# Decode attention with the roles of the score matmul swapped: row-layout softmax in place of column-layout softmax, and one slot arena

## The chip, the cores and the metric

The kernel runs on one core of one Trainium2 chip. The metric is the device time of one execution in microseconds (us); lower is better. Every quoted time is the median of the executions of that kernel. A ratio is the mean time of one kernel's fast runs over that of the other's in the same rounds, so it is not quite the ratio of the medians quoted. The span of a trace is first to last instruction. Runs are "fast" if they lie within 1.5% of the fastest of the same kernel.

## The reference

```
x = A_x                                   # 4 batches, 1 token, D = 512
x = x + attention(layernorm(x))           # layer 0
x = x + glu(layernorm(x))                 # layer 1
x = x + attention(layernorm(x))           # layer 2, same K and V
x = x + glu(layernorm(x))                 # layer 3

attention: q = x @ wq                     # 32 query heads of 128, 8 KV heads
           k, v = the last 2048 positions of the caches, each KV head for 4 query heads
           p = softmax(q k^T / sqrt(128)); o = p v; return o @ wo
glu:       h = sigmoid(x @ w_gate) * (x @ w_up); return h @ w_down     # F = 1792
```

All tensors are bf16. One pair (batch, KV head) has a K block and a V block of 512 KB each, 32 of both. With four batches of one token, everything is matrix times a few columns, and 73.9 MB come from HBM (V twice, because the kernel keeps only K between the layers).

## The kernel before

The program lists logical operations with their reads and writes. A list scheduler with a cost model turns the list into one fixed order per engine, and semaphores are worked out from it. So the order on each engine is static: an engine that reaches an instruction whose input is missing waits, even if a later one could run.

K is loaded position-major and transposed on TensorE (PE) in layer 0. The transposed K stays in SBUF for layer 2. Buffers are: 32 places for transposed K, a place for the whole output projection, and an arena of 9 slots of 512 KB for everything else. In layer 2 a K place becomes a slot once its scores are done.

Scores in column layout: K^T is stationary, q moves (4 columns), so a block needs 16 weight loads and 16 tiny matmuls, and positions lie on partitions:

```
for j in range(NJ):                                   # 16 blocks of 128 positions
    c0 = b * NJ * REP + j * REP
    last = pe.matmul(ps[:, sbk, c0:c0 + REP],
                     kt[:, i * SLOT + j * 128: i * SLOT + (j + 1) * 128],       # stationary 128x128
                     qT[:, b * HQ + h * REP: b * HQ + (h + 1) * REP],           # 4 columns
                     start=True, stop=True)
# ... softmax across partitions, cut here: max over j (DVE), fp32 transpose (PE), max (DVE),
# broadcast (DVE), transpose back (PE), copy (ACT), subtract (DVE), exp (ACT) -> ebuf, sum (DVE),
# sum over partitions with a matrix of ones (PE), reciprocal (DVE)
for j in range(NJ):                                   # P times V
    last = pe.matmul(ps[:, OB, b * REP:(b + 1) * REP], src[:, j * 128:(j + 1) * 128],
                     ebuf[:, c0:c0 + REP], start=(j == 0), stop=(j == NJ - 1))
# ... scale by the reciprocal (DVE), output projection WO (16 matmuls), add to x (DVE)
```

Of the kernel before, what the change touches and what calls it, by code (L numbers as in the profile page):

```python
# [6 lines left out]
F32 = mybir.dt.float32  # L7
BF16 = mybir.dt.bfloat16
ACTF = mybir.ActivationFunctionType
ALU = mybir.AluOpType  # L10
# [234 lines left out]
class _SlotPool:  # L245

    def __init__(self, slots, est=None):
        self.free = [(s, ()) for s in slots]
        self.est = est

    def alloc(self):
        if not self.free:
            raise RuntimeError("slot pool exhausted (logical op order needs more slots)")
        if self.est is None:
            return self.free.pop(0)[0]
        best = 0
        best_t = None
        for k, (s, names) in enumerate(self.free):
            t = 0.0
            for n in names:  # L260
                v = self.est.get(n, 0.0)
                if v > t:
                    t = v
            if best_t is None or t < best_t - 1e-9:
                best, best_t = k, t
        return self.free.pop(best)[0]

    def release(self, s, names=()):
        self.free.append((s, tuple(names)))
# [3 lines left out]
    sem_lat=120.0, pick_tol=60.0,  # L273
    dma_issue=450.0, dma_lat0=900.0, dma_lat1=1100.0, dma_max_out=8,
    bw_4k=338.0, bw_1k=292.0, bw_8k=350.0,
    pe_pair=33.0, pe_tr=107.0, pe_small=230.0, pe_f32=590.0,
    dve_fix=70.0, dve_f32=1.04, dve_bf_psum=0.52,
    act_fix=70.0, act_el=0.833,
# [3 lines left out]
def build(nc, A_x, A_k, A_v, A_wq, A_wo, B_wg, B_wu, B_wd, out, cfg=None):  # L282
# [3 lines left out]
    NA = cfg.get("NA", 9)  # L286
    NE = cfg.get("NE", 4)
    ND = cfg.get("ND", 2)
# [11 lines left out]
    assert SQ == 1 and DH == 128 and D % 128 == 0 and W % 128 == 0 and F % 128 == 0  # L300
    assert HQ == HKV * REP and A_wq.shape[0] == D and A_wo.shape[0] == HQ * DH and A_wo.shape[1] == D
    SLOT = NJ * 128
    GC = NB * NJ * REP
    NR = NB * REP
    NX = NC * NB
    NBLK = NB * HKV
    TB = min(8, NJ)
    NHALF = NJ // TB
    assert NJ % TB == 0 and GC <= 512 and NR <= 128 and HQ * NB <= 512 and NFC * NB <= 512
    assert NB <= 32 and SLOT >= D  # L310
    SCALE = float(DH) ** -0.5
    EPS = 1e-5
    WOH = REP * D
    HQC = max(1, min(HQ, SLOT // 128))
    NQCH = (HQ + HQC - 1) // HQC
    GCW = max(128, min(F, (SLOT // 128) * 128))
    NGCH = (F + GCW - 1) // GCW
    FCC = max(1, SLOT // D)
    NDCH = (NFC + FCC - 1) // FCC

# [12 lines left out]
    with es:  # L333
        def sb(name, shape, dt):
            return es.enter_context(nc.sbuf_tensor(name, shape, dt))

        kt = sb("kt", [128, NBLK * SLOT], BF16)
        wo_sb = sb("wo_sb", [128, HKV * WOH], BF16)
        arena = sb("arena", [128, NA * SLOT], BF16)
        ident_b = sb("ident_b", [128, 128], BF16)  # L340
        ident_f = sb("ident_f", [128, 128], F32)
        ones_f = sb("ones_f", [128, 128], F32)
        x_nat = sb("x_nat", [NB, D], BF16)
        o_nat = x_nat
        xT = sb("xT", [128, NX], F32)
        xc = sb("xc", [128, NX], F32)
        sq = sb("sq", [128, NX], F32)
        xn = sb("xn", [128, NX], BF16)
        lnl = sb("lnl", [128, NB], F32)
        lr1 = sb("lr1", [128, NB], F32)  # L350
        lr2 = sb("lr2", [128, NB], F32)
        xb16 = sb("xb16", [128, NX], BF16)
        rstd = sb("rstd", [128, NB], F32)
        qT = sb("qT", [128, NB * HQ], BF16)
        m1 = sb("m1", [128, ND * NR], F32)
        gmv = sb("gmv", [NR, ND], F32)
        Gb = sb("Gb", [NR, ND * 128], F32)
        gbc = sb("gbc", [128, ND * NR], F32)
        dbuf = sb("dbuf", [128, ND * GC], F32)
        ebuf = sb("ebuf", [128, NE * GC], BF16)  # L360
        esum = sb("esum", [128, ND * NR], F32)
        rinv = sb("rinv", [128, NE * NR], F32)
        onb = sb("onb", [128, 2 * NR], BF16)
        eg = sb("eg", [128, NFC * NB], F32)
        sg = sb("sg", [128, NFC * NB], F32)
        hT = sb("hT", [128, NFC * NB], BF16)
        ps = es.enter_context(nc.psum_tensor("ps", [128, 8, 512], F32))
# [4 lines left out]
        slot_est = cfg.get("slot_est")  # L372
        for _pass in range(cfg.get("passes", 1)):
            P = _Plan()
            pool = _SlotPool(range(NA), slot_est)

            def slot_ap(s):
                if s < NA:
                    return arena[:, s * SLOT:(s + 1) * SLOT]
                i = s - NA  # L380
                return kt[:, i * SLOT:(i + 1) * SLOT]

            def slot_tok(s):
                if s < NA:
                    return (("slot", s),)
                i = s - NA
                return tuple(("kt", i, t) for t in range(NHALF))

            def bankf(b):
                return ps[:, b, :]  # L390

            def bankb(b):
                return ps[:, b, :].bitcast(BF16)

            def c_dve(n, rate=None):
                return tm["dve_fix"] + n * (tm["dve_f32"] if rate is None else rate)

            def c_act(n):
                return tm["act_fix"] + n * tm["act_el"]

            def c_pairs(n):
                return n * tm["pe_pair"]

            def dma(name, dst, src, w, r=(), rate="bw_4k", nbytes=None, sem=None):
                if nbytes is None:
                    nbytes = dst.partition_size() * dst.free_nbytes()
                o = P.op("sync", name, 0.0, lambda e, dst=dst, src=src: e.dma_start(dst, src),
                         r=r, w=w, dma_bytes=nbytes, dma_rate=tm[rate])
                if sem is not None:
                    o.sem = sem  # L410
                    o.inc = 16
                return o

            P.op("gpsimd", "ones", 200.0, lambda g: g.memset(ones_f[:], 1.0), w=[("ones_f",)])
            P.op("gpsimd", "ident_f", 300.0,
                 lambda g: g.affine_select(ident_f[:], ones_f[:], [[1, 128]], ALU.is_equal, 0.0,
                                           base=0, channel_multiplier=-1),
                 r=[("ones_f",)], w=[("ident_f",)])
            P.op("gpsimd", "ident_b", 200.0, lambda g: g.tensor_copy(ident_b[:], ident_f[:]),
                 r=[("ident_f",)], w=[("ident_b",)])  # L420

            QB = cfg.get("QB", 7)
            dma("x_in", x_nat[:, :], x_d, w=[("xnat",)], rate="bw_1k")

            def emit_xT_in(t):
                last = None
                for c in range(NC):
                    last = t.transpose(bankb(QB)[:, c * NB:(c + 1) * NB], x_nat[0:NB, c * 128:(c + 1) * 128],
                                       ident_b[0:NB, 0:NB])
                return last  # L430
            P.op("tensor", "xT_tr", NC * tm["pe_small"], emit_xT_in, r=[("xnat",), ("ident_b",)],
                 w=[("psx", QB)], banks=(QB,))
            P.op("vector", "xT_cp", c_dve(NX), lambda v: v.tensor_copy(xT[:, :], bankb(QB)[:, 0:NX]),
                 r=[("psx", QB)], w=[("xT",)], banks=(QB,))

            def layer_norm(L):
                def e_bsum(t, src, dst):
                    return t.matmul(dst, ones_f[:, :], src, start=True, stop=True)
                P.op("vector", "ln_r1_%d" % L, c_dve(NX),
                     lambda v: v.tensor_reduce(lr1[:, :], xT[:, :].rearrange("p (c b) -> p b c", c=NC), AXX, ALU.add),  # L440
                     r=[("xT",)], w=[("lr1",)])
                P.op("tensor", "ln_sum%d" % L, tm["pe_f32"], lambda t: e_bsum(t, lr1[:, :], ps[:, QB, 0:NB]),
                     r=[("lr1",), ("ones_f",)], w=[("pss", QB)], banks=(QB,))
                P.op("vector", "ln_center%d" % L, c_dve(NX),
                     lambda v: v.scalar_tensor_tensor(
                         xc[:, :].rearrange("p (c b) -> p c b", c=NC),
                         ps[:, QB, 0:NB].unsqueeze(1).broadcast_to([128, NC, NB]),
                         -1.0 / D,
                         xT[:, :].rearrange("p (c b) -> p c b", c=NC),
                         ALU.mult, ALU.add),  # L450
                     r=[("pss", QB), ("xT",)], w=[("xc",)], banks=(QB,))
                P.op("vector", "ln_sq%d" % L, c_dve(NX),
                     lambda v: v.tensor_tensor(sq[:, :], xc[:, :], xc[:, :], ALU.mult),
                     r=[("xc",)], w=[("sq",)])
                P.op("vector", "ln_r2_%d" % L, c_dve(NX),
# [23 lines left out]
            def attention(L, first, banks):  # L479
# [38 lines left out]
                if first:  # L518
                    k_head(0)
# [326 lines left out]
```

## Time and profile before

219.12 us, median of 3 (218.67 to 220.54).

The times of stages here and below are starts of operations in the trace.

| stage (trace before) | us from the span's start |
|---|---|
| last residual of layer 0's attention | 120.7 |
| q of layer 2 ready | 143.2 |
| last residual of layer 2's attention | 202.2 |
| last weight packet landed | 198.2 |
| end of span | 215.5 |

From the page of the kernel before: busy time by engine, then busy tenths in 40 slices of 5.4 us, the granted PE clock, the bytes moved, the DMA queues. Then three groups: K^T scores (L561), P times V (L636), the first maximum (L572), each as "busy us, mean ns | idle time before, what ended it".

```profile
span 215.5 us, 7541 instructions
PE 152.5 (71%) x3496; PEld 142.9 (66%) x3496; DVE 68.0 (32%) x193; ACT 44.2 (20%) x75; POOL 1.0 (0%) x7
...
PE   2944869879696987969673574657758777676664
...
PEclk9995595785759585575955555555555555555555
...
GB/s 206 332 418 411 408 392 405 395 407 396 400 400 393 401 394 379 309 415 341 368 398 289 270 316 324 420 408 406 407 409 408 408 411 403 403 379 174 3 3 1
...
q8 instruction: 27, 0.44, 0.8%
...
L561 PE MATMUL ps<-qT,kt 128*128 128x4 bf16 x1024 | 32.7, 166 | 11.6 <-DVE dbuf L594 5.1
...
L636 PE MATMUL ps<-ebuf,arena 128*128 128x4 bf16 x800 | 25.7, 166 | 4.1 <-issue 2.9
...
L572 DVE TENSOR_REDUCE m<-ps 128x16 f32<-128x256 f32 x16 | 6.7, 422 | 12.7 <-PE ps L561 12.7
```

Slices that nothing disturbs move about 408 GB/s. At that rate 73.9 MB need 181 us, an estimate of the least time without loading less. Three places keep the kernel from it: the start, the dip in slices 16 to 24 (counted from 0), and the time after the last load.

The chain of waits of the kernel before, in layer 2 (start us, us, what), shows one more thing.

```profile
156.81 1.26 PE ps L636 x48
...
159.16 2.64 issue
161.80 0.37 PE ps L575
...
165.51 1.15 PE ps L636 x44
166.66 1.33 issue
168.00 0.70 PE ps L636 x20
...
172.27 0.59 PE ps L636 x23
172.86 1.32 issue
```

"Issue" is time for which the profile shows no reason. Here it falls inside groups of 16 P-times-V matmuls that share one semaphore wait (after 44 = 16 + 16 + 12 of them), so it is no wait for data. It comes back every 6 to 7.5 us, and so do the 16 KB packets of the instruction queue: between 139.8 and 190.5 us they start 6.1 to 6.8 us apart. Each of these nine packets is followed by one issue wait of PE (0.8 to 2.9 us), and each wait ends 2.4 to 2.7 us after its packet starts. 27 packets for 6992 matmuls and weight loads of PE come to 259 each. That PE waits for its instructions there is the author's inference from these times; before_no_v2 below tests it.

### The profile page before, as it was taken

The page shows a single profiled execution, that of the slowest core. Times are in us where ns is not written, and L with a number is a line of the kernel's source. Part 1 is how long each engine was busy: PE and PEld are TensorE (multiplying, and loading weights), DVE is VectorE, ACT ScalarE, POOL GpSimd, SP SyncE. Part 2 cuts the span into 40 slices and gives each one's busy share as a digit, 9 for nine tenths or more (in the row PEclk, how much of TensorE's full clock was granted, in tenths as well). Part 3 has the DMA queues.
Part 4 walks back from the last instruction along what each step waited for, and adds up shares of the span by engine and source line. Part 5 has one row for each costly group of instructions (what it writes and reads, how often), then busy time and mean ns, then how long its engine had stood idle before and what let it go on. Part 6 is the DMA issues. An engine that isn't in the chain of part 4 may idle for free.

```text
span 215.5 us, 7541 instructions
## 1 busy us (share of the span) xinstructions
PE 152.5 (71%) x3496; PEld 142.9 (66%) x3496; DVE 68.0 (32%) x193; ACT 44.2 (20%) x75; POOL 1.0 (0%) x7
## 2 busy tenths in 40 slices
PE   2944869879696987969673574657758777676664
PEld 2933859779595987959563573546757776566563
DVE  1400353433435343343513211013313422433121
ACT  2610251615325151532501000001101100101000
POOL 1000000000000000000000000000000000000000
PEclk9995595785759585575955555555555555555555
DMA  6999999999999999999997899999999999995000
GB/s 206 332 418 411 408 392 405 395 407 396 400 400 393 401 394 379 309 415 341 368 398 289 270 316 324 420 408 406 407 409 408 408 411 403 403 379 174 3 3 1
DMA packets 26447, 74.42 MB, mean 345 GB/s; under 512 B 2344, under 2 KB 10032, under 8 KB 26416
## 3 DMA queue, kind: packets, MB, share of 16 engines
q1 hardware_dynamic: 26416, 73.94, 90.2%
q8 instruction: 27, 0.44, 0.8%
q14 instruction: 4, 0.03, 0.0%
HBM read 73.93 MB, written 0.00 MB: 343 GB/s over the span
## 4 chain that ended last, share of the span: by engine, by line
PE 60%; DMA 13%; DVE 12%; issue 10%; ACT 3%; SPq 0%; DVEq 0%
PE ps L501 21%; PE ps L636 13%; PE ps L561 10%; DMA arena<-in_A_wq_dram 9%; PE ps L611 3%; PE ps L657 3%; DVE dbuf L594 3%; DVE m L572 3%; DMA arena<-in_B_w_down_dram 2%; PE ps L575 2%; PE ps L586 2%; PE ps L695 2%; DMA arena<-in_A_k_cache_dram 2%; PE ps L737 1%; DVE Gb L583 1%
## 5 line engine op out<-in xcount | busy, mean ns | idle before, releaser
L501 PE MATMUL ps<-ident_b,arena 128*128 128x128 bf16 x512 | 47.5, 279 | 1.1 <-DMA arena<-in_A_k_cache_dram 1.1
L501 PEld LDWEIGHTS ps<-ident_b,arena 128*128 128x128 bf16 x512 | 45.2, 131 | 1.3 <-DMA arena<-in_A_k_cache_dram 1.1
L514 ACT COPY kt<-ps 128x1024 bf16<-128x1024 bf16 x32 | 31.5, 1015 | 49.9 <-PE ps L501 49.9
L561 PEld LDWEIGHTS ps<-qT,kt 128*128 128x128 bf16 x1024 | 30.6, 102 | 15.9 <-issue 7.8
L561 PE MATMUL ps<-qT,kt 128*128 128x4 bf16 x1024 | 32.7, 166 | 11.6 <-DVE dbuf L594 5.1
L510 DVE COPY kt<-ps 128x1024 bf16<-128x1024 bf16 x32 | 22.1, 692 | 27.1 <-PE ps L501 27.1
L636 PEld LDWEIGHTS ps<-ebuf,arena 128*128 128x128 bf16 x800 | 25.9, 106 | 4.9 <-issue 4.4
L636 PE MATMUL ps<-ebuf,arena 128*128 128x4 bf16 x800 | 25.7, 166 | 4.1 <-issue 2.9
L590 ACT COPY gbc<-ps 128x16 f32<-128x16 f32 x16 | 2.8, 172 | 73.0 <-PE ps L586 73.0
L533 PE MATMUL ps<-xn,arena 128*128 128x4 bf16 x256 | 9.3, 166 | 9.9 <-DMA arena<-in_A_wq_dram 7.6
L533 PEld LDWEIGHTS ps<-xn,arena 128*128 128x128 bf16 x256 | 8.0, 102 | 11.3 <-DMA arena<-in_A_wq_dram 8.9
L657 PE MATMUL ps<-onb,wo_sb 128*128 128x4 bf16 x256 | 9.5, 167 | 2.2 <-issue 1.2
L572 DVE TENSOR_REDUCE m<-ps 128x16 f32<-128x256 f32 x16 | 6.7, 422 | 12.7 <-PE ps L561 12.7
L575 PE MATMUL ps<-ident_f,m 128*16 128x128 f32 x16 | 5.3, 334 | 7.4 <-DVE m L572 4.1
L657 PEld LDWEIGHTS ps<-onb,wo_sb 128*128 128x128 bf16 x256 | 8.7, 106 | 2.5 <-issue 1.7
L611 PE MATMUL ps<-esum,ones_f 128*128 128x16 f32 x32 | 8.7, 350 | 2.1 <-DVE esum L606 2.1
L636 PE MATMUL ps<-ebuf,kt 128*128 128x4 bf16 x224 | 7.4, 166 | 3.5 <-issue 3.1
L636 PEld LDWEIGHTS ps<-ebuf,kt 128*128 128x128 bf16 x224 | 7.1, 106 | 4.0 <-issue 3.9
L594 DVE TENSOR_TENSOR dbuf<-ps,gbc 128x256 f32<-128x256 f32 x16 | 6.8, 425 | 9.3 <-ACT gbc L590 9.3
L611 PEld LDWEIGHTS ps<-esum,ones_f 128*128 128x128 f32 x32 | 7.4, 286 | 2.4 <-issue 1.6
L606 DVE TENSOR_REDUCE esum<-ebuf 128x16 f32<-128x256 bf16 x16 | 6.7, 420 | 6.4 <-ACT ebuf L602 6.3
L647 DVE TENSOR_TENSOR onb<-ps,rinv 128x16 bf16<-128x16 f32 x16 | 3.1, 193 | 16.8 <-PE ps L636 16.6
(46 smaller groups left out, 73.9 us busy)
## 6 DMA issues: line engine op xcount, KB each, us to landing
arena<-in_A_v_cache_dram SPq DMA_DIRECT2D x50, 512.0 KB, 9.1
arena<-in_A_k_cache_dram SPq DMA_DIRECT2D x32, 512.0 KB, 8.9
arena<-in_A_wq_dram SPq DMA_DIRECT2D x16, 512.0 KB, 9.6
kt<-in_A_v_cache_dram SPq DMA_DIRECT2D x14, 512.0 KB, 14.1
wo_sb<-in_A_wo_dram SPq DMA_DIRECT2D x8, 512.0 KB, 9.5
arena<-in_B_w_gate_dram SPq DMA_DIRECT2D x5, 448.0 KB, 8.8
arena<-in_B_w_up_dram SPq DMA_DIRECT2D x5, 448.0 KB, 7.1
arena<-in_B_w_down_dram SPq DMA_DIRECT2D x4, 512.0 KB, 5.9
```

Of the source, the lines that this page charges most:

```text
L501: last = pe.transpose(bankb(bank)[:, jj * 128:(jj + 1) * 128], src[:, j * 128:(j + 1) * 128], ident_b[:, :])
L510: lambda v, dst=dst, bank=bank: v.tensor_copy(dst, bankb(bank)[:, 0:TB * 128]),
L514: lambda a, dst=dst, bank=bank: a.copy(dst, bankb(bank)[:, 0:TB * 128]),
L533: last = pe.matmul(ps[:, QB, q * NB:(q + 1) * NB], src[:, (q - q0) * 128:(q - q0 + 1) * 128], xn[:, ktc * NB:(ktc + 1) * NB], start=(st an ...
L561: last = pe.matmul(ps[:, sbk, c0:c0 + REP], kt[:, i * SLOT + j * 128: i * SLOT + (j + 1) * 128], qT[:, b * HQ + h * REP: b * HQ + (h + 1) ...
L572: lambda v, S4=S4, m1v=m1v: v.tensor_reduce(m1v.rearrange("p (b r) -> p b r", b=NB), S4, AXX, ALU.max),
L575: lambda pe, m1v=m1v, mbk=mbk: pe.transpose(ps[0:NR, mbk, 0:128], m1v, ident_f[:, :]),
L594: lambda v, dv=dv, gbv=gbv, S_all=S_all: v.tensor_tensor(dv.rearrange("p (b j r) -> p b j r", b=NB, j=NJ, r=REP), S_all.rearrange("p (b j ...
L606: lambda v, ev=ev, esv=esv: v.tensor_reduce(esv.rearrange("p (b r) -> p b r", b=NB), ev.rearrange("p (b j r) -> p b r j", b=NB, j=NJ, r=RE ...
L611: lambda pe, esv=esv, mbk=mbk: pe.matmul(ps[:, mbk, 256:256 + NR], ones_f[:, :], esv, start=True, stop=True),
L636: last = pe.matmul(ps[:, OB, b * REP:(b + 1) * REP], src[:, j * 128:(j + 1) * 128], ebuf[:, c0:c0 + REP], start=(j == 0), stop=(j == NJ - 1))
L657: last = pe.matmul(ps[:, OB, 64 + c * NB: 64 + (c + 1) * NB], wo_sb[:, h * WOH + r_ * D + c * 128: h * WOH + r_ * D + (c + 1) * 128], ov[: ...
```

## The change

The intent: fewer, larger score matmuls, a softmax along the free axis, and one pool of buffers. Now q is stationary (4 columns) and K^T moves, 512 positions at a time. The four batches write to partitions 0, 32, 64 and 96, which is meant to let their matmuls run side by side. A row of 2048 scores fills PSUM banks 0 to 3. Softmax is one maximum over the row (DVE), two exponentials with row sums (ACT). P then lies in rows and is turned back to columns by matmuls with a 0/1 selection matrix. In layer 2 heads go in pairs, with q padded by zeros so that two heads share the banks.

The diff, cut to its core (new names and the rest of the softmax are left out where marked):

```
-        kt = sb("kt", [128, NBLK * SLOT], BF16)
-        wo_sb = sb("wo_sb", [128, HKV * WOH], BF16)
-        arena = sb("arena", [128, NA * SLOT], BF16)          # 9 slots
+        arena = sb("arena", [128, NS * SLOT], BF16)          # 49 slots; K is transposed in place
...
+        def scores_softmax(L, heads, ptb, smb):
...
+            for c in range(NCH):                             # 4 chunks of 512 positions, bank c
...
+                    for i, h in enumerate(heads):
+                        for b in range(NB):
...
+                            last = pe.matmul(ps[32 * b:32 * b + rows, c, :], qt[:, q0:q0 + rows],
+                                             slot_ap(s)[:, c * CH:(c + 1) * CH],
+                                             start=(i == 0), stop=(i == ni - 1))
...
+            P.op("vector", "mx%d_%d" % (L, heads[0]), c_dve(SLOT),
+                 lambda v: v.tensor_reduce(nm, ps[:, 0:NCH, :].rearrange("p c n -> p (c n)"), AXX, ALU.max, negate=True),
+                 r=[("pss", c) for c in range(NCH)], w=[("nm", k2)], banks=tuple(range(NCH)))
+            for t in range(2):
+                P.op("scalar", "ex%d_%d_%d" % (L, heads[0], t), ...,      # exp of 1024, with row sum
...
+                def e_pt(pe, t=t):
...
+                    for j in range(8 * t, 8 * t + 8):
+                        last = pe.matmul(ps[:, ptb, j * n:(j + 1) * n], prow[:, j * 128:(j + 1) * 128], sel_b[:, 0:n], ...)
...
-                T=[(0, "vector"), (2, "scalar"), (1, "vector"), (3, "scalar")], S=[4], M=[6], O=5)))
+                    bank, ev = (4, "vector") if tcount[0] % 2 == 0 else (5, "scalar")     # transposes: 2 banks, not 4
...
+        units2 = [order2[i:i + 2] for i in range(0, HKV, 2)]   # layer 2: pairs of heads, from 7 down
```

Layer norm also changes, from two fp32 sums over partitions to one. V is still loaded twice (the new parameter for keeping some of it, KEEP_V, is 0).

## The prediction

> **What bounds the kernel now.** Three things in turn. (1) The whole-execution page: 73.9 MB are read and a full slice moves about 408 GB/s, so DMA alone needs 181 us; nothing in the change removes a byte (KEEP_V is 0, V is still read twice). (2) First attention layer: the chain of waits runs through PE (transposes alone 21% of the span), one head takes about 12.2 us against 11.6 us of DMA (4.7 MB). At its end the nine-slot arena lets DMA fall to 270-370 GB/s in slices 16-24 (86-130 us): about 9 us lost. (3) Second attention layer: 7.2 us a head. The chain shows "issue" waits of 1.1-2.6 us about every 6.2 us, and the instruction queue's 16 KB packets start 6.2-6.3 us apart. [...] A head has about 300 PE instructions, 1.17 blocks x 6.2 = 7.3 us: the layer runs at the fetch rate. So PE finishes late: last weights land about 195 us, the span ends at 215.5, a 20 us tail.
>
> **What changes.**
> - Scores: 1024 pairs (32 ns each) become 256 matmuls of 512 columns[...] PE instructions fall from about 7000 to 5700; the second layer from about 300 to 210 a head.
> - Added: 192 selection matmuls (about 0.5 us a head).
> - Removed: per head two small fp32 transposes, the subtraction, the two strided reductions.
> - Softmax: one 2048-wide DVE maximum (estimate 2.3 us, from 422 ns for 256), two 1024-wide exps (about 1.1 us, from the 1015 ns copy), a 0.4 us copy. The chain from scores to PV grows from about 3 to 6 us. In layer 0 the next head's transposes cover it; they get two PSUM banks instead of four.
> - 49 slots in one arena: DMA runs ahead from the start; K slots return after each pair of heads.
> - Layer norm: one fp32 sum instead of two, about 1 us less, exposed twice or thrice.
>
> **Critical path.** Layer 0 head period 11.6-12.2 us, close to DMA: its last output projection moves from 120.7 to about 113. The dip at 86-130 us mostly closes. After that 30 MB remain, 73 us. Second layer: 420 instructions a pair of heads x 24 ns = 10.2 us, about equal to its V traffic (10.3), so 41-46 us instead of 58. Loads end about 186 instead of 195; tail about 9 us instead of 20. Span about 195, plus the 3.6 us between span and timed run.
>
> Predicted: **199 us, 8 in 10 within 191 to 209**. Faster by over 2%: 0.91; within 2%: 0.06; slower: 0.03.
>
> **Right if:** DMA holds 400+ GB/s through 80-130 us; PE instructions near 5700, instruction packets 27 to about 22-23; layer-2 heads at about 5.2 us; score matmuls averaging at most 110 ns; tail after the last load under 12 us; mean DVE maximum about 2.3 us, off the chain in layer 0.
>
> **Wrong if:** [...] layer 0's transposes stall because the long maximum and exps hold DVE and ACT while only two banks turn (head period 13+ us, total 207+); the deeper DMA queue lengthens instruction fetch beyond 6.2 us; or the second layer becomes bound by its serial chain scores-maximum-exp (about 8 us a pair plus PV).

Passages that no trace of this case shows are cut from it: how the matmuls of the four batches were to come to run side by side, the estimate of the score time that rested on it, the first of four risks (that these matmuls run one after another instead), and a statement on instruction blocks from elsewhere. The sum came to a span of about 195 us, and with the 3.6 us to 199. The 110 ns under "right if" were the upper end of that estimate and rest on no trace; 128 ns, four pairs at 32 ns, would have saved PE nothing. The 1.17 blocks and the 24 ns agree with the 259 instructions a packet measured above: 300 / 259 x 6.2 us is 7.2 us a head, and 6.2 us / 259 is 24 ns. The 0.5 us of the selection matmuls is 16 at 32 ns. The 2.3 us need a second point beside the 422 ns for 256: the other maximum of that trace took 278 ns for 128 (L579, on 16 partitions), and the line through both gives 2.4 us, an estimate.

## The result, and the profile after

209.69 us, median of 4 (208.48 to 211.49), against 218.89 us; ratio 0.963, 95% interval 0.956 to 0.970. It is faster, but by 9.2 us and not by the 20 that 199 us would have meant, and the time lies just above the range that ended at 209.

| stage | before | foretold | after |
|---|---|---|---|
| last residual of layer 0's attention | 120.7 | about 113 | 118.5 |
| q of layer 2 ready | 143.2 | (not given) | 141.9 |
| layer 2's attention, from there to its last residual | 59.0 | 41 to 46 | 53.4 |
| last weight packet landed | 198.2 (read as 195) | about 186 | 195.6 |
| end of span | 215.5 | about 195 | 207.9 |

The same lines of the page, of the changed kernel (scores are L598 in both forms, P times V L659, the maximum L607, the exponentials L611).

```profile
span 207.9 us, 6311 instructions
PE 143.3 (69%) x2872; PEld 110.4 (53%) x2872; DVE 71.7 (35%) x155; ACT 67.1 (32%) x103; POOL 1.4 (1%) x9
...
PE   1684885969969499797756662547296972967564
...
PEclk9955588596699676969975555555555555555555
...
GB/s 204 348 414 412 411 391 408 398 405 404 392 408 390 407 394 405 402 395 411 391 363 261 240 359 300 419 409 407 408 409 408 411 404 407 406 405 368 121 3 1
...
q8 instruction: 22, 0.36, 0.7%
...
L611 ACT ACTIVATE prow<-ps,nmax 128x1024 bf16<-128x1024 f32 x24 | 26.6, 1113 | 46.7 <-DVE nmax L607 46.6
L659 PE MATMUL ps<-ebuf,arena 128*128 128x4 bf16 x1024 | 29.5, 166 | 7.4 <-DVE xT L691 5.2
...
L607 DVE TENSOR_REDUCE nmax<-ps 128x1 f32<-128x2048 f32 x12 | 27.5, 2290 | 11.8 <-PE ps L598 11.8
...
L598 PE MATMUL ps<-arena,qpad 128*8 128x512 bf16 x128 | 15.5, 617 | 0.8 <-DVE qpad L577 0.8
...
L598 PE MATMUL ps<-arena,qflat 128*4 128x512 bf16 x128 | 13.8, 481 | 0.5 <-DVE qflat L565 0.5
```

The operations themselves cost about what was foretold. Scores take 29 us of PE. In the trace four score matmuls of the four batches start within 10 ns of each other (142.680 to 142.690 us), and each next four 0.38 to 0.43 us later, at a granted clock of 0.50; by these starts four of them do run side by side. The maximum takes 2.29 us, an exponential 1.11. PE's matmuls fall from 3496 to 2872, the instruction packets from 27 to 22.

What is new stands in the chain of waits at the end of layer 0, after the last transposes:

```profile
101.60 0.47 PE ps L526 x8
102.07 0.56 PE ps L598 x8
...
102.66 2.30 DVE nmax L607
...
104.98 1.21 ACT prow L611 x2
...
106.24 0.36 PE ps L619 x8
106.60 0.95 PE ps L598 x8
...
109.51 2.30 DVE nmax L607
...
111.84 2.31 ACT prow L611 x4
...
115.71 1.86 PE ps L659 x64
...
117.94 0.58 PE ps L684 x16
```

Heads 6 and 7 have no next head whose transposes could fill PE. Maximum and exponentials stand one after the other in the chain, twice. The DMA queue's timeline (start us, us, what is issued) shows what that does to loading: between 102.4 and 110.0 us, and again between 111.8 and 116.3, it issues nothing. The trace puts its waits down to P times V (L659), 18.3 us in all between 98 and 122 us: slots of V that those heads still hold.

```profile
100.84 1.57 SPq L367 DMA_DIRECT2D arena<-in_B_w_gate_dram  x1
110.01 0.33 SPq L367 DMA_DIRECT2D arena<-in_B_w_up_dram  x1
...
111.33 0.43 SPq L367 DMA_DIRECT2D arena<-in_B_w_gate_dram  x1
116.31 0.33 SPq L367 DMA_DIRECT2D arena<-in_B_w_up_dram  x1
```

And the PE timeline of layer 2 (start us, us, line, what, and in brackets the idle time before and what ended it):

```profile
142.68 3.59 PE L598 MATMUL ps<-arena,qpad 128*8 128x512 bf16 x32 [0.81 <-DVE qpad L577]
149.97 0.40 PE L619 MATMUL ps<-sel_b,prow 128*128 128x32 bf16 x8 [3.70 <-ACT prow L611]
...
159.23 1.85 PE L659 MATMUL ps<-ebuf,arena 128*128 128x4 bf16 x64 [2.05 <-DVE xT L691]
...
164.33 1.03 PE L598 MATMUL ps<-arena,qpad 128*8 128x512 bf16 x8
...
171.36 1.03 PE L598 MATMUL ps<-arena,qpad 128*8 128x512 bf16 x8
176.08 0.40 PE L619 MATMUL ps<-sel_b,prow 128*128 128x32 bf16 x8 [3.69 <-ACT prow L611]
...
185.34 1.84 PE L659 MATMUL ps<-ebuf,arena 128*128 128x4 bf16 x64 [2.05 <-DVE xT L691]
```

The four longest idle times of PE, once per pair of heads and 11.5 us in all, are these: 3.7 us for maximum and exponential, or 2.05 us because the tiny residual addition (0.16 us, DVE, "xT L691") is queued behind the 2.29 us maximum. The scores of the third pair are spread over 164.3 to 172.4 us, between other work, although their banks had been free since 161.2; so the third maximum starts at 172.4. If only the 2.29 us of the maximum were taken out of the two long gaps, and the two waits behind it went away, this order would gain 2 x 2.29 + 2 x 2.05 = 8.7 us: an estimate from these lines.

### The profile page after: what moved, and what is told of

It is laid out like the page before. It is cut to its first block, busy times and chain, and to the rows that moved or that the text cites. A ratio compares the mean times of both kernels' runs of the same rounds, so it can differ in the third digit from the quotient of the medians.

```text
span 207.9 us, 6311 instructions
## 1 busy us (share of the span) xinstructions
PE 143.3 (69%) x2872; PEld 110.4 (53%) x2872; DVE 71.7 (35%) x155; ACT 67.1 (32%) x103; POOL 1.4 (1%) x9
## 4 chain that ended last, share of the span: by engine, by line
PE 36%; SPq 24%; DMA 16%; DVE 12%; ACT 7%; issue 4%; ACTq 0%; DVEq 0%
SPq L367 24%; PE ps L598 10%; PE ps L659 9%; DVE nmax L607 8%; DMA arena<-in_A_k_cache_dram 8%; PE ps L526 7%; DMA arena<-in_A_wq_dram 5%; ACT prow L611 5%; DMA arena<-in_B_w_down_dram 4%; PE ps L684 2%; PE ps L619 2%; PE ps L710 2%; PE ps L639 2%; PE ps L740 1%; ACT arena L537 1%
## 5 line engine op out<-in xcount | busy, mean ns | idle before, releaser
L526 PE MATMUL ps<-ident_b,arena 128*128 128x128 bf16 x512 | 48.5, 260 | 12.3 <-ACT arena L537 5.0
L526 PEld LDWEIGHTS ps<-ident_b,arena 128*128 128x128 bf16 x512 | 39.4, 119 | 22.3 <-issue 10.5
L537 ACT COPY arena<-ps 128x1024 bf16<-128x1024 bf16 x32 | 32.4, 1011 | 45.8 <-PE ps L526 45.8
L611 ACT ACTIVATE prow<-ps,nmax 128x1024 bf16<-128x1024 f32 x24 | 26.6, 1113 | 46.7 <-DVE nmax L607 46.6
L659 PE MATMUL ps<-ebuf,arena 128*128 128x4 bf16 x1024 | 29.5, 166 | 7.4 <-DVE xT L691 5.2
L659 PEld LDWEIGHTS ps<-ebuf,arena 128*128 128x128 bf16 x1024 | 28.6, 102 | 11.1 <-issue 11.0
L607 DVE TENSOR_REDUCE nmax<-ps 128x1 f32<-128x2048 f32 x12 | 27.5, 2290 | 11.8 <-PE ps L598 11.8
L533 DVE COPY arena<-ps 128x1024 bf16<-128x1024 bf16 x32 | 22.1, 689 | 26.8 <-PE ps L526 26.8
L619 PE MATMUL ps<-sel_b,prow 128*128 128x16 bf16 (+1 forms) x192 | 8.9, 178 | 15.2 <-ACT prow L611 15.0
L619 PEld LDWEIGHTS ps<-sel_b,prow 128*128 128x128 bf16 x192 | 7.0, 101 | 21.9 <-ACT prow L611 17.9
L598 PE MATMUL ps<-arena,qpad 128*8 128x512 bf16 x128 | 15.5, 617 | 0.8 <-DVE qpad L577 0.8
L598 PE MATMUL ps<-arena,qflat 128*4 128x512 bf16 x128 | 13.8, 481 | 0.5 <-DVE qflat L565 0.5
L684 PEld LDWEIGHTS ps<-onb,arena 128*128 128x128 bf16 x256 | 8.4, 104 | 5.6 <-DVE onb L671 4.1
L684 PE MATMUL ps<-onb,arena 128*128 128x4 bf16 x256 | 9.3, 167 | 1.7 <-DVE onb L671 1.7
## 6 DMA issues: line engine op xcount, KB each, us to landing
arena<-in_A_v_cache_dram SPq DMA_DIRECT2D x64, 512.0 KB, 12.3
```

The source lines that it names most:

```text
L526: last = pe.transpose(bankb(bank)[:, j * 128:(j + 1) * 128], half[:, j * 128:(j + 1) * 128], ident_b[:, :])
L533: lambda v, half=half, bank=bank: v.tensor_copy(half, bankb(bank)[:, 0:TB * 128]),
L537: lambda a, half=half, bank=bank: a.copy(half, bankb(bank)[:, 0:TB * 128]),
L598: last = pe.matmul(ps[32 * b:32 * b + rows, c, :], qt[:, q0:q0 + rows], slot_ap(s)[:, c * CH:(c + 1) * CH], start=(i == 0), stop=(i == ni ...
L607: lambda v: v.tensor_reduce(nm, ps[:, 0:NCH, :].rearrange("p c n -> p (c n)"), AXX, ALU.max, negate=True),
L611: lambda a, t=t: a.activation(prow[:, t * 1024:(t + 1) * 1024], ps[:, 2 * t:2 * t + 2, :].rearrange("p c n -> p (c n)"), ACTF.Exp, bias=nm ...
```

## The experiments

Two theories and a third reading were on the table.

- **Theory C, the chain**: scores, maximum and exponentials use one set of four banks, and where no other PE work is at hand (last heads of layer 0, all of layer 2) they stand in series. Form 1: the static order makes it worse. Form 2: the length of the maximum makes it.
- **Rival S, slots**: the arena is full at the end of layer 0, DMA stops, and all that follows is late.
- **Rival F, feed**: layer 2 is paced by DMA and instruction fetch, as before the change.

The edits are shown shortened. An edit that changes the cost of an operation also gives the list scheduler another order. By the traces, after_no_v2, free_wo and two_pools keep the PE order of the changed kernel, and so do no_max_l0 in layer 2 and no_max_l2 before it; all other layers that were edited got a new one. So no run takes the maximum out of an unchanged order.

All twelve in one table. Stages and spans are from the trace of one execution each, times are medians (for the unchanged pair see above). "Layer 2" is from q ready to the last residual, a difference of rounded figures, so its last digit can be off by one.

| run | layer 0 ends | q of layer 2 | layer 2 | last load | span | time us | ratio to before |
|---|---|---|---|---|---|---|---|
| changed kernel | 118.5 | 141.9 | 53.4 | 195.6 | 207.9 | 209.69 | 0.963 |
| no_max | 112.0 | 136.5 | 43.1 | 191.5 | 195.6 | 197.42 | 0.909 |
| free_wo | 120.0 | 140.1 | 52.8 | 191.4 | 205.5 | 206.70 | 0.952 |
| after_no_v2 | 122.2 | 144.8 | 49.8 | 179.4 | 207.2 | 208.90 (once) | - |
| same_group | 120.2 | 142.7 | 49.2 | 197.8 | 204.7 | 206.41 (once) | - |
| scores_first | 115.4 | 137.4 | 51.6 | 192.4 | 201.7 | 202.83 | 0.932 |
| split_max | 119.0 | 141.5 | 45.5 | 196.6 | 200.7 | 202.51 | 0.933 |
| first_split | 112.9 | 137.1 | 47.7 | 192.0 | 197.5 | 198.59 | 0.913 |
| no_max_l0 | 111.8 | 136.3 | 53.0 | 191.3 | 202.0 | 202.90 | 0.933 |
| no_max_l2 | 118.8 | 141.0 | 42.5 | 196.1 | 200.3 | 203.10 (fast runs 201.97) | 0.935 |
| two_pools | 118.2 | 141.2 | 53.2 | 195.4 | 207.1 | 210.49 | 0.967 |
| keep2 | 111.9 | 136.2 | 47.5 | 188.5 | 196.4 | 197.59 | 0.910 |
| before_no_v2 | 120.2 | 143.3 | 48.5 | 180.2 | 205.1 | 206.86 (once) | - |

The kernel before took 217.06 to 217.35 us (medians) beside them. Half the widths of the 95% intervals of the ratios lie between 0.003 and 0.008.

A warning on correctness: the comparison with the reference passed for all of them, also for the three that compute with wrong V or wrong output weights on purpose. With these inputs the comparison does not see the attention's part of the result, so "correct" is weak evidence here.

### no_max: the maximum taken away

```
-            P.op("vector", "mx...", tensor_reduce(nm, 2048 scores, max, negate=True))
+            if u < 2: P.op("vector", "mx...", memset(nm, 0.0))
```

> The changed kernel with the maximum taken away (the bias of the exponentials is a constant 0; scores are small, so the result should stay right). Theory C (the serial chain scores - 2.3 us maximum - two exponentials on one set of four score banks is what the missing gain went into): second attention layer (end of q projection to last residual) falls from 53 us to 43-46 us, the last output projection of layer 0 moves from 118.5 to about 113, total 196-201 us, ratio to before about 0.90-0.92. Rival S (the full slot arena stops DMA at the end of layer 0 and everything after it is late): the second layer keeps its 53 us, total falls by at most 3 us. Rival F (instruction fetch and DMA pace the second layer): second layer stays at 50 us or more.

Measured: 197.42 us, ratio 0.909 (0.906 to 0.913). Layer 2 takes 43.1 us, layer 0 ends at 112.0. All of theory C's numbers were met. S and F are out as the main cause, since no slot was added and no load changed. How much of the gain the new order brings is not isolated. The dip of DMA goes away by itself:

```profile
span 195.6 us, 6299 instructions
...
GB/s 199 309 409 413 410 406 394 405 393 403 400 399 409 387 405 395 404 406 392 407 393 398 396 400 360 395 410 407 407 410 407 405 410 405 407 407 406 379 229 22
```

No slice of the bytes line is under 360 between the first two and the last two, and only 4.1 us lie between the last load (191.5) and the end of the span. The span is what the prediction had taken for the changed kernel (195), but partly by luck: it had the last load at 186 and a tail of 9 us, and the two errors cancel.

### free_wo: eight more slots at the end of layer 0 (wrong result)

```
-            if L == 2:
-                done(name)                 # output projection's slot held until layer 2
+            done(name)                     # given back at once; layer 2 multiplies by the last V slot
```

> Wrong result on purpose: output-projection slots are given back after layer 0 and layer 2 multiplies by whatever lies in the last V slot, so eight more slots are free at the end of layer 0 and no byte is loaded more. Rival S: the DMA dip of 102-120 us (240-360 GB/s) closes to 400, loads of the feed-forward and of wq are there when asked for, second layer begins at 134-137 us instead of 142.7, total falls by 6-10 us. Theory C: the start of layer 2 may move by those microseconds, but the layer keeps 53 us and the last output projection of layer 0 stays at 118; if the layer is then DMA-fed later than before, the gain is under 3 us.

Measured: 206.70 us, ratio 0.952 (0.946 to 0.959), where the changed kernel has 0.963. The dip closes (392 GB/s between 110 and 120 us instead of 254), exactly as S said. But layer 2 starts only 1.8 us earlier, and the span is 2.4 us shorter (S had the start at 134 to 137 us and a total 6 to 10 us lower). With the weights there in time, the stretch from the end of layer 0 to q of layer 2 is still 20.1 us. It is now a chain of layer norm, feed-forward, layer norm and q projection on PE, with one issue wait of 2.0 us. So the stop of DMA was real but mostly covered. S is worth about 2 us alone.

### after_no_v2: layer 2 without its V loads (wrong result)

```
-                    load_kv("V2_%d_%d" % (h, b), A_v, b, h)
+                    add_load("V2_%d_%d" % (h, b), lambda s: None)
```

> Wrong result on purpose: the second layer's 16.8 MB of V are not loaded (the slots hold old data). Theory C: the second attention layer still takes 49-54 us, because its own chain sets the pace. Rival F: with DMA nearly silent the layer falls to 44 us or less and the waits called issue disappear.

Measured: 208.90 us (once); layer 2 takes 49.8 us instead of 53.4, inside what C expected. Taking 16.8 MB away saved 3.6 us of the layer. The whole hardly gained, also because layer 0, which the edit does not touch, ended 3.7 us later in this one execution (the granted clock was at half from 94.9 us to the end of that layer, in the changed kernel from 106.5; why is open). PE's order is unchanged. The one long issue wait of layer 2 (1.2 us) is gone, as F had it, but the two waits of the chain stay (engine, line, what it waited for: us in total, times, longest; 7.4 and 5.2 in the changed kernel):

```profile
PE ps L619 <- ACT prow L611: 7.4, 2, 3.7
PE ps L659 <- DVE xT L691: 4.3, 3, 2.0
```

Rival F falls as the main cause.

### same_group: the order of batches and chunks exchanged

```
-            for c in range(NCH):           # chunk outer, batch inner: neighbours of different batches
+            for g in range(2):             # batch outer, two chunks inner: neighbours of the same batch
```

> Same matmuls, other order: within half a score row the two chunks of one batch follow each other[...]. [...] a pair of chunks now costs about twice: score time on PE from 29 us to 45-60 us and the total up by 10-25 us. [...] score time stays at about 29 us and the total within 2 us.

The two forecasts are alternatives: the first if score matmuls overlap only with those of other batches next to them, the second if they do not need that.

Measured: 206.41 us (once), score time on PE 27.2 us. As a test of the overlap it failed to make what it wanted: in its trace, four score matmuls still start within 44 ns of each other (143.498 to 143.542) and the next four 0.34 to 0.38 us later. These starts lie 13 to 18 ns apart, in the changed kernel 3 to 4 ns. That would fit four batches side by side, since each batch now comes four matmuls after the last, but the kept trace does not tell which batch a matmul belongs to, so it is not shown. Overlap is shown by the starting times of the changed kernel, and not by this comparison. The total is 3.3 us lower, which neither expectation had. The order may have done that: two groups of score instructions per unit instead of four were scheduled otherwise, and layer 2 fell to 49.2 us. With one run this is a hint, no more.

### scores_first: only the order changed

```
+                o = P.op("tensor", "S%d_%d_%d" % (L, heads[0], c), ...)
+                o.prio = o.idx - 100000    # the list scheduler takes ready scores before all else
```

> Only the order of instructions changes: the score matmuls get the best priority in the list scheduler, so the next scores are issued as soon as their banks come free, ahead of P times V. Theory C, form 1 (the chain is exposed because the order issues the second half of the next scores late, behind P times V): second attention layer from 53 to 45-48 us, last output projection of layer 0 from 118.5 to 114-116, total 201-205 us, ratio to before 0.93-0.945. Form 2 (the length of the maximum itself is what counts, in any order): layer 2 stays at 51-54 us, total 207-210.

Measured: 202.83 us, ratio 0.932 (0.928 to 0.936). The total is as form 1 said, but not by the way it said. Layer 0 ends 3.1 us earlier and layer 2 starts 4.5 us earlier. Layer 2 itself stays at 51.6 us (45 to 48 expected). So order alone is worth about half of what the end of layer 0 gains without a maximum (6.7 us, no_max_l0). In layer 2 it mainly moves the idle time, as P times V comes later.

### split_max: the maximum in four pieces

```
+            for c in range(NCH):
+                P.op("vector", "mc...", tensor_reduce(cmax[:, 4*k2+c : 4*k2+c+1], ps[:, c, :], max), banks=(c,))
+            P.op("vector", "mx...", tensor_reduce(nm, cmax[:, 4*k2 : 4*k2+4], max, negate=True))
```

> The 2048-wide maximum is cut into four of 512 (about 0.69 us each, from 2.29 us for 2048 and 0.42 us for 256) that start as each score bank is done, and a small maximum of four numbers; the order of scores is left to the scheduler as in the changed kernel. Form 2 of theory C: after the last score chunk only about 0.9 us of maximum remain instead of 2.3, layer 2 falls by about 4 x 1.4 = 5.6 us to 47-48 us, layer 0 ends 2-3 us earlier, total 200-204 us. Form 1: gain under 3 us, because the scores themselves are still late.

Measured: 202.51 us, ratio 0.933 (0.930 to 0.936). A piece takes 0.69 us, the small maximum 0.15. Layer 2 falls by 7.9 us to 45.5, more than the 5.6 of form 2. In its trace the waits of PE for the exponentials fall from 7.4 to 2.3 us, and those for the residual, which no longer queues behind a maximum of 2.29 us, from 5.2 to 0.9:

```profile
PE ps L624 <- ACT prow L616: 2.3, 1, 2.3
PE ps L664 <- DVE xT L696: 0.9, 1, 0.9
```

Layer 0 does not end earlier (119.0, 2 to 3 us were expected), and the dip stays. The chain now ends in loads: the span ends 4.1 us after the last load (196.6).

### first_split: both

> Both: scores first and the maximum in four pieces. If the exposed chain is the whole of the missing gain, this comes near the run without a maximum (197.4 us): 196-201 us, second layer 42-46 us, DMA above 360 GB/s throughout 100-125 us, ratio to before 0.905-0.925, and it beats both kernels. If scheduling the scores early pushes P times V late, 201-206 us.

Its diff is the sum of the two above. Measured: 198.59 us, ratio 0.913 (0.907 to 0.918). It beats the kernel before and the changed kernel, with the maximum kept, and comes to 1.2 us from the run without any. Layer 0 ends at 112.9 and DMA never falls under 353 GB/s from the third slice of its page to the one before the last load lands. Layer 2 takes 47.7 us, outside the 42 to 46 expected. One wait of 2.29 us for an exponential is left in its first half. Its second half is no longer softmax. The PE timeline there is P times V, output projection and short waits between them, with issue waits of 2.07 and 1.28 us:

```profile
172.18 1.00 PE L665 MATMUL ps<-ebuf,arena 128*128 128x4 bf16 x32 [0.36 <-DVE xT L697]
175.24 1.01 PE L665 MATMUL ps<-ebuf,arena 128*128 128x4 bf16 x32 [2.07 <-issue]
176.54 0.58 PE L690 MATMUL ps<-onb,arena 128*128 128x4 bf16 x16 [0.29 <-DVE onb L677]
177.48 1.85 PE L665 MATMUL ps<-ebuf,arena 128*128 128x4 bf16 x64 [0.36 <-DVE xT L697]
```

Both issue waits end 2.5 to 2.6 us after an instruction packet starts (172.7 and 179.0 us), as in the kernel before, and from 152.8 us to 185.7 the packets start 6.3 to 6.8 us apart. In layer 2 of no_max, no_max_l2 and split_max they start 6.1 to 6.5 us apart as well (from 149, 152 and 157 us on). So instruction fetch, rival F, is probably the limit that comes next; no run isolates that.

### no_max_l0 and no_max_l2: the maximum taken away in one layer

```
+            if L == 0:                     # in the other run: L == 2
+                P.op("vector", "mx...", memset(nm, 0.0))
+            else: ...                      # the maximum as in the changed kernel
```

> The changed kernel without the maximum in layer 0 only, to share the 12 us of the run without any maximum between the layers. If the end of layer 0 (no transposes left to cover the chain of the last two heads) carries its part: last output projection from 118.5 to 112-114, the dip of DMA at 102-120 us closes, second layer starts 4-6 us earlier and still takes 52-54 us, total 203-206 us. If layer 0 is paced by DMA and its end by loads, no more than 2 us.

> The changed kernel without the maximum in the second layer only. If the four chains of that layer are exposed in full: the layer from 53 to 43-45 us, start unchanged near 142, total 199-202 us. If the two layers' gains do not add, because DMA becomes the limit (loads end about 188), total 202-205 us.

Measured, layer 0 alone: 202.90 us, ratio 0.933 (0.930 to 0.937). Layer 0 ends at 111.8, layer 2 starts 5.6 us earlier and still takes 53.0; the dip is gone. Layer 2 alone: 203.10 us, ratio 0.935 (0.927 to 0.942); one of its four runs counts as slow, and the three fast ones have a median of 201.97. Layer 2 takes 42.5 us and starts 0.9 us earlier; layer 0 still ends at 118.8 and the dip stays (259 GB/s between 110 and 120 us). Both stages stay just under the expected 112 to 114 and 43 to 45 us. A little of the gain in layer 2 is clock: it was granted in full from 145.0 to 151.8 us. In layer 2 of no_max, 16 score matmuls took 1.88 us at 141.1 us and 1.04 us at 143.4 us, in its stretch of full clock (143.0 to 146.4 us). In split_max and in the changed kernel it was 0.50 throughout that layer, so the 7.9 us of split_max are free of this.

In spans the two save 5.9 and 7.6 us and both together 12.3 (no_max); in medians of the fast runs 6.8, 7.7 and 12.3, in ratios 0.030, 0.029 and 0.054. (The changed kernel ran in other rounds, where the kernel before took 218.89 us and not about 217.2, so the medians flatter these runs.) In the layer-2 run the attention ends 11.8 us earlier, but about 4 us of it are lost again, because the last load lands at 196.1 and the feed-forward then waits for it. So the two costs nearly add up, and their sum is of the size of the missing gain: span 195 foretold, 207.9 measured, 195.6 without the maximum.

### two_pools: the arena divided again

```
+        pool = _SlotPool(NS - 40); held = list(range(NS - 40, NS))
+            s = held.pop(0) if holds(name) else pool.alloc()      # K and wo only from the 40
```

> The changed kernel with its 49 slots divided as the kernel before divides its buffers: 40 that only K and the output projection may take, 9 for all else until layer 2. Tests what the one arena is worth by itself. If running ahead matters: heads of layer 0 wait for V, total up 3 us or more (212+). If layer 0 is paced by the DMA rate in both kernels: within 2 us of 209.7.

Measured: 210.49 us, ratio 0.967 (0.963 to 0.972), against 0.963 (0.956 to 0.970). No difference is seen: every stage in the table is within 0.9 us. Running ahead buys nothing in layer 0, where DMA moves 392 GB/s in the old and 401 in the new kernel (20 to 100 us), and 401 again with the divided pool.

### keep2: two V blocks kept

```
-    KEEP_V = cfg.get("KEEP_V", 0)
+    KEEP_V = cfg.get("KEEP_V", 2)      # on top of first_split
```

> Scores first and the maximum in four pieces, and two V blocks of head 7 kept from layer 0 to layer 2, so 1 MB less is loaded (2.6 us at 408 GB/s), at the price of two slots fewer between the layers. If that version is now bound by DMA: 195.5-197.5 us against 198.6. If the two slots are missed more than the megabyte, or the chain still ends last: 198-201.

Measured: 197.59 us, ratio 0.910 (0.907 to 0.913), beside 0.913 (0.907 to 0.918) of first_split. That is just above the 195.5 to 197.5 us expected of a kernel bound by DMA. It is the shortest time with the maximum kept, but the intervals overlap, so whether it beats first_split is not settled. Its last load lands 3.5 us earlier and the span ends only 1.1 us earlier: first_split was not bound by loads alone.

### before_no_v2: the old layer 2 with DMA nearly silent (wrong result)

```
-                dma(name, slot_ap(s), kv_d(cache, b, h), w=slot_tok(s))
+                if not name.startswith("V2"): dma(...)
```

> The kernel before, wrong on purpose: the second layer's V is not loaded. Tests the claim of the prediction that the old second layer (7.2 us a head) runs at the rate at which instruction blocks arrive under DMA load. If so, with DMA nearly silent the blocks come closer together than 6.2 us, the issue waits of 1.1-2.6 us shrink and a head takes 6.0 us or less (layer from 59 to 48 us or less). If the old chain of softmax sets the pace, it stays at 7 us a head, 57 us or more.

Measured: 206.86 us (once). Layer 2 falls from 59.0 to 48.5 us, 6.1 us a head; the expectation (6.0, 48) was missed by a hair, the rival (7) clearly refuted. While DMA was silent the instruction packets came 3.6 to 4.8 us apart, and the chain of waits shows no issue wait over 0.2 us between 143 and 159 us. Where weights were loaded again (about 160 to 180 us) they came 8.8 and 6.3 us apart, and the issue waits were back (1.77 and 2.45 us). These two also end 2.2 to 2.5 us after a packet starts. The edit also gave PE another order in layer 2, but that does not explain the packets; the issue waits over 0.5 us fell from 12.3 us in that layer to 4.2, which is 8.1 of the 10.5 us. So, by this one run, the old layer 2 did wait for instructions, and they did wait for data traffic (packets 3.6 to 4.8 us apart without it, 6.1 to 6.8 with it).

## Why the prediction was wrong, point by point

- **Right: the operations.** Scores at 112 ns each in layer 2 where they run in one piece (32 in 3.59 us), 115 over all 256 (29.4 us; at most 110 expected, so just over), maximum 2.29 us (2.3), exponential 1.11 us (1.1), matmuls and packets as counted. The four batches do run side by side by their starts (four within 10 ns); that they might not was the first risk named.
- **Right: the old layer 2 runs at the rate of instruction fetch.** Shown by before_no_v2 (layer 2 from 59.0 to 48.5 us, packets 3.6 to 4.8 us apart instead of 6.1 to 6.8), and by the packets that start 2.4 to 2.7 us before each issue wait ends.
- **Wrong, the step that failed: "Second layer: 420 instructions a pair of heads x 24 ns = 10.2 us ... so 41-46 us instead of 58".** It measured 53.4, 13.3 us a pair. The prediction removed one limit and took the next one it had costed (fetch, DMA) for the bound, though it listed the true one under "wrong if": the serial chain scores, maximum, exponentials on one set of banks. After_no_v2 shows that feed was not the limit (49.8 us without V). Split_max and no_max_l2 show that the maximum in series was: 45.5 and 42.5 us, both with a new order; in the unchanged order the estimate is 8.7 us of the 10.9. The 42.5 are 10.6 us a pair, so the size foretold for fetch was about right; that it would be the limit was not.
- **Wrong in part: "In layer 0 the next head's transposes cover it".** Up to head 5 they do so well enough for DMA to keep its rate (401 GB/s from 20 to 100 us), though transposes wait 12.3 us in all, 1.1 before the change. For heads 6 and 7 there are none left, and the end moved to 118.5 instead of 113; two maxima of 2.30 us stand in the chain there. No_max_l0 puts it at 111.8, scores_first at 115.4, split_max leaves it at 119.0, and both of these together give 112.9.
- **Wrong: "The dip at 86-130 us mostly closes".** It moved to 104 to 130 us and is deeper (240 GB/s in the lowest slice, 270 before). Its cause was taken to be the arena; in the changed kernel it follows from the late P times V of heads 6 and 7, which holds the slots: it vanishes when the chain is shortened (no_max_l0, first_split) with the same 49 slots (eight more close it too, free_wo, but the span gains only 2.4 us). Two_pools shows no gain in time from the one arena.
- **Wrong: "tail about 9 us instead of 20".** The last load of the kernel before lands at 198.2 us, not 195, so the tail was 17.3; after the change it is 12.3.
- **Wrong, a small term: 3.6 us between span and time.** It compared the span of one execution with the median of others. Spans and times of the same execution differ by about 1.7 us, so the foretold span of 195 would have been 197, and the miss in the stages is larger than the 0.7 us by which the time left the range.
- **Where the real 7.6 us of span came from**: 2.2 us at the end of layer 0, and 5.6 us in layer 2 (59.0 to 53.4); the stretch between gave 0.9 back and the feed-forward at the end took about 0.7 less. That fewer instructions helped layer 2 fits before_no_v2, but no run here isolates it.

What stays open: why layer 2 of first_split is 2.2 us longer than of split_max, and how the 20 us between the layers divide among latency, issue waits and the clock, which was granted at 0.50 there.

What sets the granted clock is open as well. In the changed kernel's layer 2 it was 0.50 throughout, also in a 10 us window with PE busy 8.73 us (160 to 170 us; the ends of matmuls are modelled). In layer 2 of no_max and no_max_l2 it was full for 3.4 us (from 143.0) and 6.8 us (from 145.0). In layer 0, where transposes are PE's largest group, the mean was 0.78 (20 to 100 us), and 16 transposes took 1.05 us at 84.4 us, in a stretch of full clock; in the kernel before it was 0.69 in the same window.

## What to carry to other kernels

When a change removes the limit of a stage, write out the serial chain of one unit and count how many sets of buffers let two units overlap; here a longer chain with one set of banks became the next limit where no other work was left, at the end of a loop above all (no run tried a second set). A long instruction in the middle of a chain should be cut along the pieces its input arrives in, so that most of it runs while the input is still being made and small operations can pass between: here a maximum of 2.29 us in four pieces of 0.69 us took 7.9 us from layer 2 (split_max, in a new order). And a stop of DMA caused by late consumers is better mended at the consumer: here eight more slots closed it as well, but were worth 2.4 us of span, the shorter chain 5.9 (no_max_l0).
